# Thresholded attention and a feed-forward on one core: where q and k are loaded in SyncE's queue, and how the third pair's thresholds reach all partitions

## The chip, the core and the metric

The kernel runs on one core of a Trainium2 chip. Its engines work side by side, each through its own list of instructions in order: TensorE (PE; its weight loads are PEld), VectorE (DVE), ScalarE (ACT), GpSimd (POOL) and SyncE (SP), which here only issues DMAs. GpSimd issues DMAs too. An instruction waits for semaphores of others. The metric is the time of the whole program on the device in microseconds (us), the median of several runs.

## The reference

There are 8 batches of 8 heads, 576 rows of 64 each. For every head the scores are taken, all scores lower than the row's maximum minus tau are dropped, the rest go through a softmax, and the result is multiplied by v. The heads are put side by side (4608 rows of 512), and a feed-forward with a sigmoid gate follows.

```python
scores = scale * np.matmul(q, k.transpose(0, 1, 3, 2))
thresh = np.max(scores, axis=-1, keepdims=True) - tau
scores = np.where(scores >= thresh, scores, -1000000000.0)
attn = np.exp(scores - np.max(scores, axis=-1, keepdims=True))
attn = attn / (np.sum(attn, axis=-1, keepdims=True) + 1e-09)
attn_out = np.matmul(attn, v)            # then (B,H,S,D) -> (B*S, H*D) = x
h = x @ w_in                             # 512 -> 2048
g = h * (1.0 / (1.0 + np.exp(-1.702 * h)))
out = g @ w_out                          # 2048 -> 512
```

q, k, v are float32; the weights w_in and w_out come as 64-bit floats and are turned into float32 on the chip.

## The kernel before, in words

**Pairs.** Attention works on pairs of heads, 32 of them, 4 to a batch (`NPAIR` is 4, `n` the number of the pair). For pair `n`, `load_qk` brings q and k by four DMAs each into `raw0` and `raw1`, and `prep` transposes them on VectorE into `qkT` (L358). Each of these has one buffer for all pairs but 1 and 3, which have homes of their own in the arena, where the feed-forward will work later. So the load of a pair waits until the pair before it has been transposed. `scores` (L382 and, for the last 64 keys, L375) puts scores transposed into PSUM, keys on partitions, queries along the row, and `keep` (L405) copies them to SBUF on ScalarE, in four big tiles and one tail tile.

**Thresholds.** Queries lie along the row, so the maximum of a query goes over partitions. `in_groups` (L419) reduces within groups of 32 partitions, `over_tiles` and `over_groups` reduce the rest, and tau is taken off. The result must then stand on all 128 partitions, as `mb`, for the subtraction. There are two ways:

- For pairs below `BY_DMA` (8): `lower_rows` (L454, L459) forms a row in the small tile `flat`, `row_out` (L471) writes it to DRAM on SyncE's queue, and `row_in` (L480, L482) reads it back broadcast, once as `mb` and in two halves as `mbt` for the tail.
- For the others: `lower` (L443, L448) and `spread_max` (L463), a transpose of a broadcast operand on VectorE. There is no `mbt` then, and the subtraction of the tail is done in two halves (L494 instead of L491).

`sub` (L489) takes the thresholds off on VectorE, `mask` (L500) and `exps` (L504) follow on ScalarE. `values` multiplies by v (L518, tile `pv`). The sums are taken by TensorE too for the first five pairs (`sums_by_pe`, L518, tile `den`), else by VectorE. `spread_sums` and `place_x` (L585) scale and write the transposed result, `xT`.

**Weights.** w_in and w_out come in 16 pieces each, issued by GpSimd (L310, L311, 0.5 MB twice a piece) into staging places, w_in first. VectorE and ScalarE turn a piece into float32 (L321, L329, L335, L339, L347). The chain of loads goes on when a staging place is free.

**Feed-forward.** It takes blocks of 256 rows. The first two (L640, L622) can start when the four pairs of batch 0 are placed; all the others (L600, L690) use the seven products of Strassen's scheme, with sums made by GpSimd.

**Order.** The order of each engine's instructions is fixed while the program is built, by a planner. Every piece of work is a task with an engine, a planned cost, a rank, the tasks it comes `after` and the buffers it takes and gives. The planner plays time forward; a free engine takes the ready task with the lowest rank. The rank is the number of the pair plus a number of the function, `EARLY` for pairs 0 to 7 and `LATER` for the rest; the feed-forward's products have a rank behind all pairs. Planned costs have no effect but on this order. On the chip an instruction waits for what its data and buffers demand, not for the plan: an `after` without a transfer of data between the two tasks only sets their order where they lie on the same queue. Loads of q, k and v, both halves of the way through DRAM, and the stores of the output all lie on SyncE's one queue.

Of the kernel before, what the change touches and what calls it, by code (L numbers as in the profile page):

```python
# [30 lines left out]
def kernel(  # L31
# [37 lines left out]
    NPAIR = H // 2  # L69
# [59 lines left out]
    for x in ("raw0", "raw1", "qkT0", "qkT1", "mb"):  # L129
# [6 lines left out]
        "lower_rows": -1.89,  # L136
        "values": 1.63,
        "exps": 1.38,
        "load_qk": -1.15,
        "prep": -1.35,  # L140
        "load_v": 1.46,
        "mask": 0.88,
        "over_groups": -1.9,
        "sub": -0.29,
        "one_group": 0.95,
        "scores": -0.68,
        "spread_sums": 0.92,
        "sums_by_pe": 1.09,
        "in_groups": 0.61,
        "keep": -1.15,  # L150
    }
# [3 lines left out]
    }  # L155
    CV = {
        "cv_power": 0.15,
    }

    def task(engine, cost, rank, f, *a, after=(), take=(), give=(), lag=0.06):  # L160
        if 0 <= rank < LAST:
            rank += CV.get(f.__name__, 0.0) + (EARLY if a[0] < 2 * NPAIR else LATER).get(f.__name__, 0.0)
        tasks.append((engine, cost, rank, f, a, [x for x in after if x is not None],
                      take, give, lag))
        return len(tasks) - 1
# [67 lines left out]
    def own(n, *pools):  # L233
        return tuple(x + "_apart" for x in pools) if n in APART else pools
# [521 lines left out]


    BY_PE = 5
    BY_DMA = 8
    LEAD = 6  # L760
    WHOLE = 6

    FFU = 1.722

    W_IN, W_OUT = (3.21, 1.53), (3.16, 2.2)
    ready_w, w_loads = [], []
    for i in range(len(pieces)):
        if i < n_in:
# [11 lines left out]
        m = task("ACT", 0.79, rank, cv_power, i, after=[e])  # L780
# [6 lines left out]
    tau_done = task("DVE", 1.0, -2.0, tau_terms, after=[warm])  # L787


    placed, ffn = {}, []  # L790
    last_mm2, t_ready = {}, []

    def first_blocks():
# [88 lines left out]
    for n in range(NP):  # L882
        gate = per_pair * (n - LEAD)
        after = ffn[gate : gate + 1] if gate >= 0 else []
        r = float(n)

        slow = 1.2 if n < NPAIR else 1.0
        q0, q1 = (nc.sync, nc.scalar) if n == 0 else (nc.sync, nc.sync)
        lq = task("SP", 2.0, r - 2.0, load_qk, n, 0, q0, take=own(n, "raw0"), lag=2.0)
        lk = task("SP", 2.0 if n else 0.1, r - 2.0, load_qk, n, 1, q1, take=own(n, "raw1"), lag=2.0)  # L890
        v_tail = f"v_t{n % 2}"
        lv = task("SP", 2.1, r - 1.2, load_v, n, take=("v_m", v_tail), lag=2.0)
        pq = task("DVE", 0.77, r, prep, n, 0, after=[lq], take=own(n, "qkT0"), give=own(n, "raw0"))
# [8 lines left out]
        for t in range(NKT + 1):  # L902
            tail = t == NKT
            copies = []
            if tail or n >= WHOLE:
# [5 lines left out]
                    take=("psA", "s_t") if tail else ("psA", "psA") + own(n, "s_m"),  # L911
                    give=own(n, "qkT0", "qkT1") + ("kd",) if tail else (),
                )
                after = [a]
                copies = [task("ACT", 0.65, r, keep, n, t, c, after=[a], give=("psA",)) for c in cs]
            else:
                for c in range(2):
# [3 lines left out]
                        take=("psA",) + (own(n, "s_m") if c == 0 else ()),  # L921
                    )
                    after = [a]
# [1 line left out]
            mx.append(task("DVE", 0.76 if tail else 1.37, r, in_groups, n, t, ALU.max, after=copies))  # L925
        a = task("DVE", 0.78, r, over_tiles, n, ALU.max, after=mx)
        a = task("DVE", 0.78, r, over_groups, n, ALU.max, after=[a])
        if n < BY_DMA:
            a = task("DVE", 0.5, r, lower_rows, n, after=[a, tau_done], take=("row",))
            a = task("SP", 0.35, r, row_out, n, after=[a], lag=2.8)  # L930
            m = task(
                "SP", 1.5, r, row_in, n, after=[a], take=own(n, "mb") + ("mbt",), give=("row",),
                lag=5.0,
            )
        else:
            a = task("DVE", 0.7, r, lower, n, after=[a, tau_done])
            m = task("DVE", 1.38, r, spread_max, n, after=[a], take=own(n, "mb"))
        ws, subs = [], [m]
        for t in range(NKT + 1):
            tail = t == NKT  # L940
            a = task(
                "DVE", (0.76 if n < BY_DMA else 1.5) if tail else 1.36, r, sub, n, t, after=subs[-1:],
                give=own(n, "mb") + (("mbt",) if n < BY_DMA else ()) if tail else (),
            )
            subs.append(a)
            a = task("ACT", 0.68 if tail else 1.16, r, mask, n, t, after=[a])
            ws.append(task("ACT", 0.87 if tail else 1.34, r, exps, n, t, after=[a]))
        back = own(n, "s_m") * NKT + ("s_t",)
        every = range(NKT + 1)
        if n < NPAIR:  # L950

            pv = den = None
            for t in every:
# [3 lines left out]
                    take=("psM", "psM") if first else (),  # L957
# [3 lines left out]
                    take=("psA",) if first else (), give=(back[t],) if t < NKT else ("s_t", "v_m", v_tail),  # L961
# [60 lines left out]
```

## Time and profile before

| | before |
|---|---|
| time, median of 3 (lowest to highest) | 1401.76 us (1399.66 to 1402.35) |
| span of the profile | 1401.9 us |
| mean granted TensorE clock | 0.988 |
| PE busy before 140 us, and after | 89.4 us, 1251.8 us |
| VectorE busy over the span | 1037.4 us |
| ScalarE, GpSimd busy | 625.9 us, 281.7 us |
| first product of the feed-forward (L640) | 134.88 us |
| DMA over the span | 79.59 MB, 205728 packets |

In the profile "busy" is the time in which an engine has an instruction running. Lines of groups read: line of the code, engine, operation, output and input, shapes, number, then busy time and mean ns of one, then the idle time before them and what ended it. In a timeline a line is the start, the duration, the engine (SPq is SyncE's queue of DMA issues; the duration is that of the issuing, not of the transfer), and in brackets how long the engine had been idle and what it waited for. In the chain of waits a line is start, duration, and what held the end at that time.

### The profile page before, as it was taken

The numbers are of one execution on the slowest core, as the hardware profiler recorded it, in microseconds if no ns is written. First come the engines' busy times: TensorE is split into PE (matmuls) and PEld (weight loads), VectorE is DVE, ScalarE is ACT, GpSimd is POOL, SyncE is SP. The second block draws the span as 40 slices with busy tenths as digits, with TensorE's granted clock in tenths as the row PEclk, the third lists the DMA queues.
The fourth block names the chain that finished last, engine by engine and source line by source line (L and its number), as shares of the span: only waits on it lengthen the run. The fifth ranks groups of instructions, "written<-read, shape, count | busy, mean of one in ns | idle before, by whom it ended". The sixth has DMA issues, their size and how long they took to land.

```text
span 1401.9 us, 18089 instructions
## 1 busy us (share of the span) xinstructions
PE 1341.3 (96%) x6856; PEld 1012.6 (72%) x6856; DVE 1037.4 (74%) x1773; ACT 625.9 (45%) x806; POOL 281.7 (20%) x374
## 2 busy tenths in 40 slices
PE   5748999999999999999999999999999999999998
PEld 3325774467777777777777777777777778888887
DVE  7859899888888888878988888888888886111111
ACT  5647454654444545455454555543545453100100
POOL 1201223123021121212120303020212212211211
PEclk9869999999999999999999999999999999999999
DMA  8756873311111111111111111101111100000000
GB/s 181 202 176 193 248 250 92 92 25 27 41 27 41 26 34 33 26 33 26 41 26 41 24 35 26 41 17 41 26 42 26 25 9 8 8 16 15 1 15 15
DMA packets 205728, 79.59 MB, mean 57 GB/s; under 512 B 192841, under 2 KB 192841, under 8 KB 205641
## 3 DMA queue, kind: packets, MB, share of 16 engines
q1 hardware_dynamic: 196072, 44.60, 15.1%
q0 software_dynamic: 7200, 33.55, 7.1%
q8 instruction: 54, 0.88, 0.3%
q10 hardware_dynamic: 2368, 0.30, 0.2%
q14 instruction: 34, 0.27, 0.1%
HBM read 68.93 MB, written 9.47 MB: 56 GB/s over the span
## 4 chain that ended last, share of the span: by engine, by line
PE 86%; DVE 7%; DMA 4%; issue 2%; SPq 2%; ACT 0%; POOL 0%; DVEq 0%; POOLq 0%
PE hps L600 32%; PE ops L690 27%; PE pv L518 10%; PE ps L382 9%; PE ops L622 3%; PE ps L375 2%; SPq L246 2%; PE hps L640 1%; DVE s_m L489 1%; DVE part L419 1%; DMA w_out<-in_moe_w_in_dram 1%; DVE arena L489 1%; DMA arena<-row 1%; DMA arena<-in_moe_w_out_dram 1%; DMA w_out<-in_moe_w_out_dram 1%
## 5 line engine op out<-in xcount | busy, mean ns | idle before, releaser
L600 PE MATMUL hps<-xT,w_in 128*128 128x256 f32 x2048 | 457.3, 381 | 0.0
L600 PEld LDWEIGHTS hps<-xT,w_in 128*128 128x128 f32 x2048 | 385.8, 190 | 67.3 <-issue 11.3
L419 DVE TRANSPOSE_TENSOR_REDUCE part<-s_m 128x36 f32<-128x1152 f32 x228 | 304.8, 1355 | 61.6 <-ACT s_m L405 58.0
L405 ACT COPY s_m<-ps 128x576 f32<-128x576 f32 x240 | 141.1, 643 | 243.9 <-PE ps L382 240.6
L690 PE MATMUL ops<-w_out,arena 128*128 128x256 f32 x1024 | 232.8, 381 | 0.0
L690 PEld LDWEIGHTS ops<-w_out,arena 128*128 128x128 f32 x1024 | 192.8, 190 | 33.6 <-issue 6.2
L609 ACT ACTIVATE th<-hps 128x512 f32<-128x512 f32 x144 | 85.4, 593 | 294.2 <-PE hps L600 280.7
L500 ACT ACTIVATE s_m<-s_m 128x1152 f32<-128x1152 f32 x120 | 136.1, 1156 | 131.8 <-DVE s_m L489 131.0
L668 POOL TENSOR_TENSOR arena<-arena 128x256 f32<-128x256 f32 x64 | 58.5, 915 | 677.0 <-DVE arena L612 677.0
L690 PE MATMUL ops<-arena 128*128 128x256 f32 x768 | 174.3, 381 | 0.0
L489 DVE TENSOR_TENSOR s_m<-s_m,mb 128x1152 f32<-128x1152 f32 x120 | 160.9, 1374 | 16.5 <-DMA mb<-row 15.8
L612 DVE SCALAR_TENSOR_TENSOR arena<-th,hps 128x512 f32<-128x512 f32 x128 | 87.1, 680 | 111.3 <-ACT th L609 109.3
L690 PEld LDWEIGHTS ops<-arena 128*128 128x128 f32 x768 | 144.8, 190 | 24.7 <-issue 4.6
L382 PE MATMUL ps<-qkT 64*128 64x288 f32 x960 | 149.6, 435 | 10.9 <-DVE qkT L358 9.3
L504 ACT ACTIVATE s_m<-s_m,shift,scl 128x1152 f32<-128x1152 f32 x120 | 157.3, 1342 | 0.9
L382 PEld LDWEIGHTS ps<-qkT 64*128 64x128 f32 x960 | 84.2, 190 | 69.2 <-issue 32.2
L518 PE MATMUL pv<-s_m,v_m 128*64 128x288 f32 x960 | 123.1, 409 | 0.0
L712 DVE SCALAR_TENSOR_TENSOR osb<-ops,osb 128x256 f32<-128x256 f32 x112 | 44.5, 409 | 99.5 <-PE ops L690 98.5
L518 PEld LDWEIGHTS pv<-s_m,v_m 128*64 128x64 f32 x960 | 66.5, 137 | 53.0 <-issue 9.7
L622 PE MATMUL ops<-w_out,arena 128*128 128x512 f32 x128 | 59.4, 613 | 2.8 <-DVE w_out L347 2.8
L640 PE MATMUL hps<-xT,w_in 128*128 128x256 f32 x256 | 58.0, 383 | 3.5 <-DVE arena L646 2.5
L670 POOL TENSOR_TENSOR arena<-arena 128x256 f32<-128x256 f32 x64 | 60.3, 941 | 0.0
(97 smaller groups left out, 1050.3 us busy)
## 6 DMA issues: line engine op xcount, KB each, us to landing
out_dram<-osb SPq DMA_DIRECT2D x36, 256.0 KB, 2.0
q_raw<-in_q_dram SPq DMA_DIRECT2D x120, 72.0 KB, 2.2
k_raw<-in_k_dram SPq DMA_DIRECT2D x116, 72.0 KB, 2.2
v_m<-in_v_dram SPq DMA_DIRECT2D x64, 128.0 KB, 2.4
w_out<-in_moe_w_in_dram POOLq DMA_DIRECT2D x12, 512.0 KB, 9.6
arena<-in_moe_w_out_dram POOLq DMA_DIRECT2D x12, 512.0 KB, 6.0
w_out<-in_moe_w_in_dram POOLq DMA_DIRECT2D x12, 511.6 KB, 10.5
arena<-in_moe_w_out_dram POOLq DMA_DIRECT2D x12, 511.6 KB, 6.8
```

The source lines that it names most:

```text
L382: nc.tensor.matmul(ps[:, h, 0:SH], lhsT=kT[ts(h, D), ts(t, P)], rhs=qT[ts(h, D), ts(c, SH)], start=True, stop=True,)
L405: nc.scalar.copy(out=o, in_=pss.pop((n, t, c))[:, :, 0:SH])
L419: nc.vector.tensor_reduce(out=o, in_=i, axis=AXL.X, op=op, apply_transpose=True)
L489: nc.vector.tensor_tensor(out=s, in0=s, in1=mb, op=ALU.subtract)
L500: nc.scalar.activation(out=s, in_=s, func=AF.Prelu, alpha=STEEP)
L504: nc.scalar.activation(out=s, in_=s, func=AF.Exp, scale=scl, bias=shift)
L518: nc.tensor.matmul(o[c][ts(h, D), 0:SH], lhsT=lhsT, rhs=rhs, start=(t == 0), stop=(t == NKT),)
L600: nc.tensor.matmul(hidden[j][:, ts(f, BLK)], lhsT=w_in[:, c, ds((f * HF + j) * P, P)], rhs=xTs[blk][:, c, :], start=(c == 0), stop=(c == N ...
L609: nc.scalar.activation(out=ths[j], in_=hidden[j], func=AF.Tanh, scale=GELU_SCALE / 2)
L612: nc.vector.scalar_tensor_tensor(out=g[:, :, j, :], in0=two(ths.pop(j)), scalar=1.0, in1=two(hidden.pop(j)), op0=ALU.add, op1=ALU.mult,)
L622: nc.tensor.matmul(acc[i], lhsT=g0[:, j, ts(i, P)], rhs=w_out[:, j, :], start=(j == 0), stop=(j == NFC - 1),)
L690: nc.tensor.matmul(banks[k][:, ts(o, HM)], lhsT=left[:, j, :], rhs=right[:, j, :], start=(j == 0), stop=(j == HF - 1),)
```

## The change

Pair 2, the third, gets its thresholds by `spread_max` on VectorE instead of through DRAM. The loads of q and k of pair n, from pair 4 on, are planned after the thresholds of pair n-2, so that they lie behind these in SyncE's queue. It is meant to keep a long load from standing ahead of a small row that VectorE waits for. The planned cost of the loads of pairs 4 to 7 is raised, and the ranks are set anew for the first eight pairs and the weights.

```diff
     EARLY = {
         "lower_rows": -1.89,
         "values": 1.63,
         "exps": 1.38,
-        "load_qk": -1.15,
-        "prep": -1.35,
+        "load_qk": -1.72,
+        "prep": -1.69,
         "load_v": 1.46,
-        "mask": 0.88,
+        "mask": 1.64,
         "over_groups": -1.9,
-        "sub": -0.29,
+        "sub": -1.05,
         "one_group": 0.95,
-        "scores": -0.68,
-        "spread_sums": 0.92,
-        "sums_by_pe": 1.09,
+        "scores": 0.67,
+        "spread_sums": 1.4,
+        "sums_by_pe": 2.29,
         "in_groups": 0.61,
         "keep": -1.15,
     }
...
     CV = {
         "cv_power": 0.15,
+        "cv_frac": 0.13,
     }
...
-    BY_DMA = 8
+    BY_DMA = (0, 1, 3, 4, 5, 6, 7)
...
-    W_IN, W_OUT = (3.21, 1.53), (3.16, 2.2)
+    W_IN, W_OUT = (3.11, 1.53), (2.49, 2.62)
...
-    placed, ffn = {}, []
+    placed, spread, ffn = {}, {}, []
...
-        lq = task("SP", 2.0, r - 2.0, load_qk, n, 0, q0, take=own(n, "raw0"), lag=2.0)
-        lk = task("SP", 2.0 if n else 0.1, r - 2.0, load_qk, n, 1, q1, take=own(n, "raw1"), lag=2.0)
+
+        behind = [spread[n - 2]] if n >= NPAIR else []
+        cost = 3.5 if NPAIR <= n < 2 * NPAIR else 2.0
+        lq = task("SP", cost, r - 2.0, load_qk, n, 0, q0, after=behind, take=own(n, "raw0"), lag=2.0)
+        lk = task(
+            "SP", cost if n else 0.1, r - 2.0, load_qk, n, 1, q1, after=behind,
+            take=own(n, "raw1"), lag=2.0,
+        )
...
-        if n < BY_DMA:
+        if n in BY_DMA:
             a = task("DVE", 0.5, r, lower_rows, n, after=[a, tau_done], take=("row",))
             a = task("SP", 0.35, r, row_out, n, after=[a], lag=2.8)
...
             m = task("DVE", 1.38, r, spread_max, n, after=[a], take=own(n, "mb"))
+        spread[n] = m
```

The two other places that ask whether a pair's thresholds come by DMA, in the tail's `sub`, are changed likewise from `n < BY_DMA` to `n in BY_DMA`.

More of the change, by code (lines that the diff above doesn't have):

```diff
@@ L941 @@
             a = task(
-                "DVE", (0.76 if n < BY_DMA else 1.5) if tail else 1.36, r, sub, n, t, after=subs[-1:],
-                give=own(n, "mb") + (("mbt",) if n < BY_DMA else ()) if tail else (),
+                "DVE", (0.76 if n in BY_DMA else 1.5) if tail else 1.36, r, sub, n, t, after=subs[-1:],
+                give=own(n, "mb") + (("mbt",) if n in BY_DMA else ()) if tail else (),
             )
```

## The prediction

> **What bounds the kernel now.** I read the busy shares first, then the slices, then a table of stretches, then the chain of waits, then the two queues (VectorE and SyncE) around the one hole.
>
> ```profile
> span 1401.9 us, 18089 instructions
> PE 1341.3 (96%) x6856; PEld 1012.6 (72%) x6856; DVE 1037.4 (74%) x1773; ACT 625.9 (45%) x806; POOL 281.7 (20%) x374
> PE   5748999999999999999999999999999999999998
> DVE  7859899888888888878988888888888886111111
> ```
>
> The span is PE work plus PE idle: 1341.3 + 60.6. The digits put nearly all the idle into the first four slices, 140 us. The table of stretches says so in us (after the stretch: PE, PEld, DVE, ACT, POOL busy, granted clock, DMA share, GB/s):
>
> ```profile
> 0.00:60.00 60.00, 37.42 (x238) 21.68 (x240) 46.50 (x77) 40.17 (x52) 10.26 (x34) 0.94 0.75 175
> 60.00:70.00 10.00, 5.26 (x34) 2.69 (x30) 9.47 (x25) 3.04 (x6) 4.23 (x8) 0.91 1.10 286
> 70.00:80.00 10.00, 4.41 (x26) 1.94 (x24) 0.04 (x1) 0.95 (x2) 0.00 (x1) 0.84 1.04 334
> 80.00:90.00 10.00, 0.00 (x0) 0.00 (x0) 4.13 (x4) 2.64 (x3) 0.00 (x0) 0.50 0.53 123
> ...
> 140.00:230.00 90.00, 84.71 (x391) 60.39 (x390) 81.51 (x136) 48.75 (x63) 25.83 (x38) 0.99 0.73 220
> 230.00:300.00 70.00, 70.00 (x288) 32.58 (x288) 61.37 (x119) 33.24 (x41) 13.41 (x9) 0.99 0.24 63
> 300.00:1402.00 1102.00, 1097.13 (x5628) 869.00 (x5626) 786.32 (x1327) 458.24 (x592) 220.08 (x270) 1.00 0.12 26
> ```
>
> PE idles 50.6 us before 140, 5.3 from 140 to 230, nothing to 300 and 4.9 after. So the time is set by when the feed-forward starts (first L640 product at 134.88, a steady stream from 137.41, when pair 3's xT is written at 136.97), plus a nearly full PE. Before it, VectorE is the bound: up to 137.9 it is idle 31.7 us, of which 9.0 are the start (waits of 5.91 and 3.06), 3.43 one wait for pair 1's thresholds and 15.82 one for pair 2's. The chain of waits runs through that hole, SyncE's queue shows what fills it, and VectorE's row closes it:
>
> ```profile
> 70.90 7.29 SPq L246
> 78.30 3.77 DMA row<-flat
> 82.08 3.76 DMA mb<-row
> ```
> ```profile
> 59.22 4.04 SPq L246 DMA_DIRECT2D q_raw<-in_q_dram  x4
> 63.37 14.82 SPq L246 DMA_DIRECT2D k_raw<-in_k_dram  x4
> 78.30 0.53 SPq L471 DMA_DIRECT2D row<-flat  x1
> ```
> ```profile
> 62.35 0.23 DVE L459 STREAM_TRANSPOSE flat<-flat 32x64 f32<-32x64 f32 x1
> ...
> 85.87 5.16 DVE L489 TENSOR_TENSOR s_m<-s_m,mb 128x1152 f32<-128x1152 f32 x4 [15.82 <-DMA mb<-row]
> ```
>
> Pair 2's row is ready at 62.58 and goes out at 78.30: pair 5's q and k stand before it on SyncE, and their issues crawl (one takes 7.29 us; 490 ns is the usual) because the weights keep the DMA engines 104 to 110% busy there. Two trips through DRAM follow, 3.77 and 3.76. Pair 1 has the same on a small scale: its row is ready at 35.75 and leaves at 39.69, behind pair 4's k (12.95 us for four issues).
>
> **What the Trainium skill says.** "DMA: Bandwidth & Descriptors", section Anatomy of one DMA: a semaphore wait is done by the issuing sequencer ahead of the dispatch, and the engines just drain their queues. That fits: the small row DMA can't overtake the loads issued ahead of it, and two late DMAs cost their latencies one after the other. Same page, section Queues, rings and completion order: each engine goes round-robin between rows of work by packet; the trace agrees that rows share, as pair 5's k lands 12.5 us after issue in that stretch against 2.2 as the median. "VectorE: DVE Perf Modes", section The three transpose paths, has VectorE's transpose as 32x32 blocks; spread_max is one such instruction over 1152 columns, and the trace prices it: 1.37 us. "Perfetto Trace Analysis", section Optimization Strategy: in a kernel with several regimes the most-contended engine changes over time, and the gaps of the regime of interest are to be followed to the semaphore that ends them; here VectorE leads to 137 and PE after it, as the table shows.
>
> **The change part by part.**
>
> 1. Pair 2's thresholds by VectorE. Removed: the wait of 15.82, and 0.46 of lower_rows (0.231 + 0.232). Added on VectorE: lower 0.66 (0.229 + 0.252 + 0.176), spread_max 1.37, and a tail subtraction in two halves, 2 x 0.755 (median of L494) instead of 0.75. Together +0.20 + 1.37 + 0.76 = +2.33 us, all on the bound engine. It also takes pair 2's three broadcast reads off the DMA engines; I cost that at nothing, since nothing waits for it any more.
>
> 2. Loads of pair n >= 4 behind the thresholds of pair n-2. This is an order on the SyncE queue, not a new semaphore. Pair 4's loads go behind pair 1's row, so that row leaves at about 35.8 instead of 39.69, lands about 3.9 earlier, at 41.8, and VectorE comes for it at 42.1: the 3.43 wait goes. What is now queued behind a threshold is q and k of two pairs on, and behind these their transposes on VectorE (prep). Room for it in the trace: pair 4 is transposed at 58.42, its scores run only from 94.89; pair 5 at 119.96, 42 us after its last load was issued. In the later part SyncE waits 316 us in all for the raw buffers to come free anyway, and a pair takes about 36 us (one pv group to the next in the chain: 318.5, 354.1, 391.5), against some 5 to 10 for a load: nothing there.
>
> 3. Planned cost of the loads of pairs 4 to 7 3.5 instead of 2.0: only the plan, no instruction. Real times in the trace: 4.04 and 14.82, 9.75 and more under weight traffic, 2 without. The plan is nearer to the truth and still short of the bad ones.
>
> 4. New ranks (scores and sums later, subtractions, loads and transposes sooner, masks later; w_out pieces from 2.49 on instead of 3.16; cv_frac 0.13 later). No instruction is added, the order is shifted, for pairs 0 to 7 and the weights. Not seen in the trace, so from both sides. Best: 15 of 16 pieces of w_in are converted before 137 at 2.21 us each (0.42 + 0.43 + 0.69 + 0.67) and the first products need four; with all other eleven after the start it would come 24 earlier, of which perhaps half is usable, as the later products want them soon. But spread_sums of pair 3 moves behind more pieces (3.92 to 4.40), which speaks against it. Worst: scores of pairs 4 and 5, now done in PE's idle time, slide behind the start of the feed-forward: 2 x 5.66 (4.42 + 1.24 each) = 11.3. I take 0.
>
> 5. New small waits. With the hole closed, weights and thresholds are asked for sooner. DMA is 98.9 us busy before 137, so at a start near 120 it is 80% full: enough in sum, tight in places. The crowded stretch 150 to 170 shows what that looks like: five waits of VectorE on weights, 0.83 + 0.89 + 1.35 + 0.63 + 0.40 = 4.1. Bounds 0 to 8; I take 3.
>
> Sum: -15.82 - 3.43 + 2.33 + 3.0 = -13.9, on a VectorE path that sets the feed-forward's start. After the start PE is nearly full, so the earlier start passes to the end: 1401.8 - 13.9 = 1387.9, rounded **1388**. What could stop it from passing on is the last w_out piece: PE waits 2.81 for it at 227.4. The chain of weight loads stood still for 23.45 us in the hole (GpSimd waiting for a staging buffer), so it moves forward with the rest.
>
> **Rivals.**
>
> A. Half the gain is given back, by waits on q and k or on weights (5 to 8 more than I took), or by scores moved into PE's full stretch (5.7 to 11.3). For it: scores lose 1.35 in rank, and prep is planned 2 us after a load that can take 15. Against it: scores of pairs 4 and 5 are ready early in the trace, and any idle PE takes them. 1393 to 1399; middle **1396**. Chance 0.22.
>
> B. More than the sum, because the new order takes conversions off the road to the first product, 5 to 12 more. For it: eleven pieces aren't needed yet. Against: rank of spread_sums. **1379**. Chance 0.14.
>
> C. A new hole of the size of the old. The most likely place is VectorE waiting in order at prep of pair 4 or 5 for a load that crawls; all behind it, subtractions and weights, waits too. For it: the loads are started later than before and their issue took 19 us (4.04 + 14.82, pair 5) and 21 (9.75 + 6.38 + 5.22, pair 6) in full traffic. 17 + one wait of 18 to 20: 1402 to 1408, **1405**, slower. Against: loads leave the fullest stretch, 60 to 80, for 85 to 105, where DMA is at 0.32 to 0.5. Chance 0.10.
>
> D. The hole is hidden: something else sets the start, such as weights. Then within 0.2%, **1401**. Against: 15 pieces are there by 137 and four are needed, and PE and VectorE both stand in the hole. Chance 0.04.
>
> **How the numbers follow.** The forecast has 0.50, spread over 1383 to 1392. Faster takes forecast, A and B and nearly all their edges: 0.86; same 0.04; slower 0.10. The range holds the forecast (0.50), A to its far end (0.22) and the nearer half of B (0.07), 0.79 together: 1376 to 1399.
>
> **What would show it.** Right: the wait of VectorE for mb from row, 15.8, is gone, and there are 25 spread_max instead of 24; pair 1's row leaves within 1 us after its transpose; first L640 near 120; PE idle before it down to about 35; the stretch after the start as full as now. Wrong: a wait of VectorE for q_raw or k_raw over 5 us; L382 products of pairs 4 and 5 behind the first L640; a longer wait of L622 for w_out.

## The result, and the profile after

The changed kernel takes 1392.73 us (median of 4 runs, 1391.75 to 1397.4) beside 1401.63 for the kernel before: the ratio, that of the mean times as in all that follows, is 0.9945, 95% interval 0.9921 to 0.997. It is faster by 8.9 us by the medians, where 13.9 was forecast. The profiled execution spans 1391.0 us; that of the kernel before was longer than its median (1403.66 us, a span of 1401.9), so the two profiles lie 10.9 us apart.

From the page of the changed kernel, the span, the busy shares and two rows of slices:

```profile
span 1391.0 us, 18051 instructions
PE 1341.9 (96%) x6856; PEld 1015.6 (73%) x6856; DVE 1053.8 (76%) x1776; ACT 634.4 (46%) x806; POOL 295.7 (21%) x374
PE   5778999999999999999999999999999999999999
DVE  7989999978888888889888888888888887111111
```

VectorE's row has no dip in its third slice any more, and PE's third slice went from 4 to 7. The table of stretches, in the same columns as before:

```profile
0.00:60.00 60.00, 40.88 (x254) 25.20 (x256) 49.26 (x84) 42.00 (x53) 11.12 (x34) 0.91 0.78 193
60.00:70.00 10.00, 5.06 (x38) 2.73 (x35) 9.75 (x20) 9.90 (x10) 1.06 (x2) 0.87 0.69 146
70.00:80.00 10.00, 10.00 (x61) 5.09 (x60) 9.61 (x15) 6.32 (x10) 3.19 (x6) 0.79 0.73 238
80.00:90.00 10.00, 9.55 (x65) 4.72 (x62) 9.50 (x24) 5.29 (x9) 3.19 (x6) 1.00 0.86 294
...
140.00:230.00 90.00, 87.15 (x413) 56.71 (x411) 83.92 (x141) 49.68 (x64) 25.45 (x35) 1.00 0.69 219
230.00:300.00 70.00, 63.55 (x251) 34.38 (x251) 60.84 (x97) 32.57 (x37) 10.99 (x8) 0.95 0.30 67
300.00:1402.00 1102.00, 1087.57 (x5584) 860.68 (x5582) 786.80 (x1323) 461.11 (x589) 232.93 (x269) 1.00 0.12 26
```

VectorE is busy 9.61 and 9.50 us from 70 to 90, where it had 0.04 and 4.13. But 230 to 300, which was full for PE, now lacks 6.45. (The span ends at 1391.0, so the last stretch has 1091 us, not 1102.) PE's idle time, from these tables and the whole stretch to 140 (103.60 busy):

| us | before | after | difference |
|---|---|---|---|
| PE idle to 140 | 50.6 | 36.4 | -14.2 |
| 140 to 230 | 5.3 | 2.9 | -2.4 |
| 230 to 300 | 0 | 6.45 | +6.45 |
| 300 to the end | 4.8 | 3.4 | -1.4 |
| PE busy, whole span | 1341.3 | 1341.9 | +0.6 |

The sum is -10.9, the difference of the two spans. So before 140 us PE gained what was forecast, and after 230 us a new wait took nearly half of it back. In SyncE's queue (start, duration of the issues) the rows leave at once, and the loads come behind them (line numbers shift by up to six from run to run, as the edits add lines):

```profile
37.36 0.28 SPq L472 DMA_DIRECT2D row<-flat  x1
...
46.85 2.22 SPq L247 DMA_DIRECT2D q_raw<-in_q_dram  x4
49.11 11.52 SPq L247 DMA_DIRECT2D k_raw<-in_k_dram  x4
...
88.02 0.30 SPq L472 DMA_DIRECT2D row<-flat  x1
92.42 0.35 SPq L481 DMA_DIRECT2D arena<-row  x1
```

Pair 1's row goes 0.3 us after its transpose starts (37.10, 0.23 long). Pair 4's k is still slow, 11.52 for its four issues, but nothing that VectorE needs soon stands behind it. What VectorE waits for in its place, by its own timeline, is small:

```profile
96.03 5.16 DVE L490 TENSOR_TENSOR arena<-arena 128x1152 f32<-128x1152 f32 x4 [1.40 <-DMA arena<-row]
...
103.57 0.78 DVE L359 STREAM_TRANSPOSE qkT<-q_raw 128x576 f32<-128x576 f32 x1 [1.72 <-DMA q_raw<-in_q_dram]
105.59 0.78 DVE L359 STREAM_TRANSPOSE qkT<-k_raw 128x576 f32<-128x576 f32 x1 [1.24 <-DMA k_raw<-in_k_dram]
```

The new wait of PE is this, first in VectorE's timeline, then in GpSimd's, then in PE's:

```profile
269.11 0.18 DVE L438 COPY fold<-red 64x36 f32<-64x36 f32 x1
269.33 2.24 DVE L439 TENSOR_TENSOR red<-red,fold 64x36 f32<-64x36 f32 x1
271.60 2.27 DVE L438 COPY fold<-red 32x36 f32<-32x36 f32 x1
273.90 2.27 DVE L439 TENSOR_TENSOR red<-red,fold 32x36 f32<-32x36 f32 x1
276.21 2.79 DVE L558 TENSOR_SCALAR r<-red 32x18 f32<-32x18 f32 x4
...
280.21 0.95 DVE L586 TENSOR_TENSOR xT<-pv,rc 128x192 f32<-128x192 f32 x4
```
```profile
269.12 4.71 POOL L664 TENSOR_TENSOR arena<-w_out,arena 128x1024 f32<-128x1024 f32 x2
273.78 4.64 POOL L664 TENSOR_TENSOR w_out<-w_out 128x1024 f32<-128x1024 f32 x2
```
```profile
281.31 2.29 PE L383 MATMUL ps<-qkT 64*128 64x288 f32 x8 [6.45 <-DVE xT L586]
283.53 3.11 PE L623 MATMUL ops<-w_out,arena 128*128 128x512 f32 x4
```

Tiny operations of VectorE, which take 0.17 to 0.19 elsewhere (four of L558 together 0.71), last as long as one of GpSimd's sums of w_out, 2.3 us, each; of the four of L558, by their total of 2.79, only one can. They belong to pair 7's sums; pair 7 is placed some 8 us late (2.24 + 2.27 + 2.27 + 2.79, less the 1.25 they take alone), and PE stands for 6.45: the next scores wait for a PSUM place that pair 7's `place_x` (L586) gives back. The granted clock is 1.00 from 269 to 275, 0.83 from 275 to 281 and 0.60 from 281 to 287, and the next twelve products take 2.29 + 3.11 where the same ones take 1.24 + 1.98 before the wait: 2.2 more. The Trainium skill has it in "SBUF — State Buffer", section SBUF: two separate sides: VectorE and GpSimd share a pair of ports under an exclusive lock, held for a whole instruction; the forms of VectorE that need the pair are those with two inputs in SBUF (against a GpSimd instruction that reads SBUF) and those in a mode that uses two ports. These rows agree in length, 2.24 to 2.27 beside sums of 2.3, and L439, with its two inputs, is of the first form; in which mode the copies and scalar operations ran, the trace doesn't say.

### The profile page after: what moved, and what is told of

It is laid out like the page before. It is cut to its first block, busy times and chain, and to the rows that moved or that the text cites. A ratio compares the mean times of both kernels' runs of the same rounds, so it can differ in the third digit from the quotient of the medians.

```text
span 1391.0 us, 18051 instructions
## 1 busy us (share of the span) xinstructions
PE 1341.9 (96%) x6856; PEld 1015.6 (73%) x6856; DVE 1053.8 (76%) x1776; ACT 634.4 (46%) x806; POOL 295.7 (21%) x374
## 4 chain that ended last, share of the span: by engine, by line
PE 85%; DVE 9%; DMA 2%; SPq 1%; issue 1%; ACT 0%; POOL 0%; DVEq 0%; ACTq 0%; POOLq 0%
PE hps L601 32%; PE ops L691 28%; PE pv L519 9%; PE ps L383 8%; PE hps L641 4%; DVE part L420 2%; PE ps L376 2%; DVE s_m L490 1%; SPq L247 1%; PE den L519 1%; DMA arena<-in_moe_w_out_dram 1%; DVE arena L340 1%; DVE red L439 1%; DMA v_m<-in_v_dram 1%; DVE w_in L348 0%
## 5 line engine op out<-in xcount | busy, mean ns | idle before, releaser
L601 PE MATMUL hps<-xT,w_in 128*128 128x256 f32 x2048 | 457.5, 381 | 0.0
L691 PEld LDWEIGHTS ops<-w_out,arena 128*128 128x128 f32 x1024 | 192.3, 190 | 36.1 <-issue 10.4
L669 POOL TENSOR_TENSOR arena<-arena 128x256 f32<-128x256 f32 x64 | 52.0, 812 | 610.8 <-DVE arena L613 610.8
L490 DVE TENSOR_TENSOR s_m<-s_m,mb 128x1152 f32<-128x1152 f32 x120 | 180.3, 1540 | 0.8
L691 PE MATMUL ops<-arena 128*128 128x256 f32 x768 | 171.0, 379 | 0.0
L613 DVE SCALAR_TENSOR_TENSOR arena<-th,hps 128x512 f32<-128x512 f32 x128 | 85.8, 671 | 100.9 <-ACT th L610 100.9
L676 POOL TENSOR_TENSOR arena<-arena 128x512 f32<-128x512 f32 x32 | 62.6, 1963 | 111.2 <-PE ops L691 111.2
L671 POOL TENSOR_TENSOR arena<-arena 128x256 f32<-128x256 f32 x64 | 60.1, 938 | 0.0
```

The costliest lines, as they stand in the source:

```text
L490: nc.vector.tensor_tensor(out=s, in0=s, in1=mb, op=ALU.subtract)
L601: nc.tensor.matmul(hidden[j][:, ts(f, BLK)], lhsT=w_in[:, c, ds((f * HF + j) * P, P)], rhs=xTs[blk][:, c, :], start=(c == 0), stop=(c == N ...
L613: nc.vector.scalar_tensor_tensor(out=g[:, :, j, :], in0=two(ths.pop(j)), scalar=1.0, in1=two(hidden.pop(j)), op0=ALU.add, op1=ALU.mult,)
L676: nc.gpsimd.tensor_tensor(out=u, in0=a12, in1=u, op=ALU.subtract)
L691: nc.tensor.matmul(banks[k][:, ts(o, HM)], lhsT=left[:, j, :], rhs=right[:, j, :], start=(j == 0), stop=(j == HF - 1),)
```

## The experiments

The loads and ranks are named as in the change. The ratio is to the kernel before, run beside each, with its 95% interval; start is that of the first feed-forward product on PE (L640 in the kernel before), in the one profiled execution of each run. The planner makes the order anew for every run: e1 to e4 differ from the kernel before, e7 and e8 from the changed kernel and e12 from e9 in the places of many other tasks too, on TensorE as well. Only e5 and e6 keep the order of the changed kernel on every engine, and e9, e10 and e11 those of e2, e1 and e4, but for the added copies. With the same order the start still differs by 0.5 to 3.4 us (123.14, 125.67 and 122.24; 121.45 and 124.73; 128.87 and 128.35; 136.26 and 137.47), so smaller differences of the start say nothing.

| run | what | us | ratio | interval | start |
|---|---|---|---|---|---|
| after | the change | 1392.73 | 0.9945 | 0.9921 to 0.997 | 123.14 |
| e1 | both parts, old ranks | 1388.5 | 0.9902 | 0.9887 to 0.9917 | 128.87 |
| e2 | VectorE alone, old ranks | 1387.0 | 0.99 | 0.988 to 0.992 | 121.45 |
| e3 | order of loads alone, old ranks | 1390.58 | 0.9916 | 0.9901 to 0.9931 | 124.78 |
| e4 | new ranks alone | 1416.68 | 1.0104 | 1.0086 to 1.0123 | 136.26 |
| e5 | the change, later sums | 1384.37 | 0.9874 | 0.9858 to 0.9891 | 125.67 |
| e6 | e5, first sums later too | 1385.11 | 0.9879 | 0.9864 to 0.9895 | 122.24 |
| e7 | the change without VectorE's part | 1403.7 | 1.0011 | 1.0003 to 1.0019 | 129.88 |
| e8 | the change without the order of loads | 1396.21 | 0.9954 | 0.994 to 0.9969 | 121.89 |
| e9 | e2, later sums | 1390.8 | 0.9924 | 0.9911 to 0.9937 | 124.73 |
| e10 | e1, later sums | 1397.88 | 0.9974 | 0.9966 to 0.9983 | 128.35 |
| e11 | e4, later sums | 1405.8 | 1.0035 | 1.0022 to 1.0049 | 137.47 |
| e12 | e9, pair 1 by VectorE too | 1399.65 | 0.9988 | 0.998 to 0.9997 | 128.51 |

### Which part makes the gain: e1 to e4

e1 is the kernel before with everything of the change but the ranks:

```diff
-    BY_DMA = 8
+    BY_DMA = (0, 1, 3, 4, 5, 6, 7)
...
+        behind = [spread[n - 2]] if n >= NPAIR else []
+        cost = 3.5 if NPAIR <= n < 2 * NPAIR else 2.0
```

> The kernel before with pair 2 spread by VectorE and the loads behind the thresholds, ranks as before. Theory Q (the queue makes the gain: the row no longer stands behind a load): both waits of VectorE on rows (15.8 and 3.4) are gone, the first L640 product comes at 120 to 125 instead of 134.9, the time is 1385 to 1393. Theory R (the new ranks make it): the start stays at 133 or later, 1397 or more.

The two waits on rows are gone and the time is as expected, but the start is not: 128.87. VectorE waits for loads instead, as its timeline shows for pair 5 (and 3.40 more for pair 4's k):

```profile
109.18 0.78 DVE L358 STREAM_TRANSPOSE qkT<-q_raw 128x576 f32<-128x576 f32 x1 [6.30 <-DMA q_raw<-in_q_dram]
111.19 0.78 DVE L358 STREAM_TRANSPOSE qkT<-k_raw 128x576 f32<-128x576 f32 x1 [1.23 <-DMA k_raw<-in_k_dram]
```

10.9 us together: the wait that the prediction's rival C had, at half its size. e1 is faster than the whole change all the same: PE idles 41.5 us before 140 (36.4 in the changed kernel), but nothing is lost from 230 to 300, where PE is full.

e2 has the first part of that diff alone:

```diff
-    BY_DMA = 8
+    BY_DMA = (0, 1, 3, 4, 5, 6, 7)
```

> The kernel before with pair 2 spread by VectorE alone; loads and ranks as before. Theory Q: the wait of 15.8 is gone, that of pair 1 (3.4) stays, 2.3 us of VectorE work are added: start at 124 to 128, time 1388 to 1395. Theory R: start at 133 or later, 1397 or more.

0.99, a little better than expected; start 121.45. Pair 1's wait is there as expected, 3.64. So this one part makes as much as both.

e3 has the other part alone:

```diff
+        behind = [spread[n - 2]] if n >= NPAIR else []
+        cost = 3.5 if NPAIR <= n < 2 * NPAIR else 2.0
```

> The kernel before with the loads behind the thresholds alone; pair 2 goes through DRAM still, ranks as before. Theory Q: pair 2's row leaves within 2 us of its transpose, and what VectorE waits for it falls from 15.8 to 0 to 5, pair 1's 3.4 goes: start at 119 to 127, time 1384 to 1394, so that the spreading by VectorE isn't needed for most of the gain. Rival: pair 4's load, now late, stops VectorE at its transpose in turn, for 5 or more: 1394 to 1402. Theory R: 1397 or more.

0.9916, start 124.78. Pair 2's row leaves at 59.44, yet VectorE waits 8.00 for it, more than expected: the trip through DRAM itself takes long in the weights' traffic (59.44 to 73.65; the DMA share is 1.01 from 59 to 74). SyncE's queue, and VectorE's row:

```profile
59.44 0.30 SPq L471 DMA_DIRECT2D row<-flat  x1
65.78 0.36 SPq L480 DMA_DIRECT2D mb<-row  x1
```
```profile
73.65 5.17 DVE L489 TENSOR_TENSOR s_m<-s_m,mb 128x1152 f32<-128x1152 f32 x4 [8.00 <-DMA mb<-row]
```

e1, e2 and e3 overlap in their intervals: the two parts are two cures of one hole, and their gains don't add.

e4 has the ranks alone (`EARLY`, `CV`, `W_IN`, `W_OUT` as in the change):

```diff
-        "scores": -0.68,
+        "scores": 0.67,
...
-    W_IN, W_OUT = (3.21, 1.53), (3.16, 2.2)
+    W_IN, W_OUT = (3.11, 1.53), (2.49, 2.62)
```

> The kernel before with the new ranks alone. Theory Q: loads of pair 4 or 5 still lie ahead of rows of pairs 1 and 2, a wait of VectorE on a row of 8 or more remains; 1396 to 1406. Theory R: the waits are filled with other work, start at 128 or earlier, 1385 to 1393.

Slower by 1.04%, worse than either theory had. The hole is where it was, in VectorE's timeline of this run:

```profile
82.32 5.17 DVE L490 TENSOR_TENSOR s_m<-s_m,mb 128x1152 f32<-128x1152 f32 x4 [15.62 <-DMA mb<-row]
```

and the same four small operations take 2.24, 2.26, 2.28 and 2.79 beside GpSimd's sums; PE waits 6.35, and the granted clock is 0.91 from 230 to 300.

### The collision: e5 and e6

e5 makes the third and fourth sum wait for pair 7:

```diff
     def t_sum(x, k):
         o, a, b = (y[:, ts(k, 4), :] for y in T_SUMS[x])
+        if (x, k) == (2, 0):
+            nc.gpsimd.tensor_copy(out=late, in_=xTs[2][:, NPAIR - 1, 128:129])
...
+        if n == 2 * NPAIR - 1:
+            tasks[t_ready[4]][5].append(placed[n])
```

> The changed kernel with one GpSimd instruction more: ahead of the third and fourth of the sums of w_out (L664) it copies one column of xT that pair 7's place_x writes, so these sums can't run before pair 7 is placed; every other instruction and its order as in the changed kernel. Theory C (GpSimd's sums at 269 to 278 hold up VectorE's small operations of pair 7, four of them at 2.2 to 2.8 us instead of 0.2 to 0.7, and so PE for 6.45): these operations take 0.2 again, pair 7 is placed 8 to 9 earlier, the PE wait of 6.45 and the slow clock behind it go: 6 to 9 less than the changed kernel, 1382 to 1387. Rival S (PE would wait there anyway, for scores moved behind the start, or VectorE is late by itself): 0 to 2 less.

1384.37: 8.4 less than the changed kernel, and the intervals are apart (0.9858 to 0.9891, and 0.9921 to 0.997). VectorE's timeline, and GpSimd's under it:

```profile
271.50 0.19 DVE L440 TENSOR_TENSOR red<-red,fold 64x36 f32<-64x36 f32 x1
...
272.14 0.71 DVE L559 TENSOR_SCALAR r<-red 32x18 f32<-32x18 f32 x4
...
275.88 1.38 DVE L421 TRANSPOSE_TENSOR_REDUCE part<-s_m 128x36 f32<-128x1152 f32 x1 [0.86 <-ACT s_m L407]
278.96 1.38 DVE L421 TRANSPOSE_TENSOR_REDUCE part<-s_m 128x36 f32<-128x1152 f32 x1 [1.71 <-ACT s_m L407]
```
```profile
274.79 4.67 POOL L667 TENSOR_TENSOR arena<-w_out,arena 128x1024 f32<-128x1024 f32 x2
```

The small operations are back at 0.19 and 0.71. The sums now lie beside transposing reductions, which take 1.38 as they do alone: this kind isn't held up. PE is full from 230 to 300, as the stretch says:

```profile
230.00:300.00 70.00, 70.00 (x288) 39.76 (x285) 61.29 (x107) 39.16 (x46) 13.21 (x10) 1.00 0.29 67
```

The start was 2.5 later in this execution than in that of the changed kernel, at the same order, and the median is still the shortest of all runs (that of e6 beside it within the noise). The two profiled executions are 6.6 us apart, of which the wait is 6.45; the 8.4 of the medians also takes in what these two don't show.

e6 does the same with the first two sums:

```diff
+        if (x, k) == (0, 0):
+            nc.gpsimd.tensor_copy(out=late, in_=w_out[:, NFC - 1, 0:1])
```

> As the run before, and the first two sums also wait, by a copy of one column of the last piece of w_out, until that is converted. Theory C: L336 and L340 of the last piece take 0.4 and 0.7 instead of 2.60 and 2.73 and the wait of L623 for it (1.61) goes: 1 to 3 less than the run before. Rival: the sums then hold up other VectorE work right behind it, and nothing is won: within 1 of it.

The wait for the last piece of w_out is gone, but two of L432 and one of L439 of a pair take 3.83 and 2.28 in turn (0.36 and 0.18 alone), and PE waits 3.20 there. 0.9879 and 0.9874: nothing won.

### The change less one part: e7 and e8

e7 is the change with `BY_DMA` over all eight pairs again (the comparisons read `n < BY_DMA` as before):

```diff
-    BY_DMA = (0, 1, 3, 4, 5, 6, 7)
+    BY_DMA = 8
```

> The changed kernel with pair 2 through DRAM again; loads behind the thresholds and new ranks stay. If spreading by VectorE does a needed part: the row's two trips in the weights' traffic (up to 3.8 each) stop VectorE for 3 to 8 and pair 4's load comes that much later, 1394 to 1401. If the order in the queue is enough: VectorE saves 2.3, 1386 to 1393.

1.0011, slower than expected, and by about 0.1% slower than the kernel before. The waits are of the kinds named, in VectorE's timeline:

```profile
68.36 5.17 DVE L490 TENSOR_TENSOR s_m<-s_m,mb 128x1152 f32<-128x1152 f32 x4 [5.88 <-DMA mb<-row]
...
104.32 5.17 DVE L490 TENSOR_TENSOR arena<-arena 128x1152 f32<-128x1152 f32 x4 [3.03 <-DMA arena<-row]
```

with 1.99 + 1.71 for pair 4's q and k between; start 129.88, and the collision is there too (PE waits 5.06). With the new ranks the change wins nothing without VectorE's part.

e8 takes the order of the loads out of the change:

```diff
-        lq = task("SP", cost, r - 2.0, load_qk, n, 0, q0, after=behind, take=own(n, "raw0"), lag=2.0)
+        lq = task("SP", 2.0, r - 2.0, load_qk, n, 0, q0, take=own(n, "raw0"), lag=2.0)
```

(and `lk` likewise).

> The changed kernel with the loads free to go ahead of the thresholds again (and at the old planned cost); pair 2 by VectorE and new ranks stay. Theory Q: a wait on a row behind a load comes back, for pair 1 (k of pair 4 lies right behind row 0, ahead of row 1) at 3 to 8 us: 1393 to 1402. If the order in the queue does nothing beside the spreading: within 3 of the changed kernel.

Pair 1's wait comes back, 3.18, but the waits for q and k go, and the start is the same, 121.89. 0.9954 and 0.9945 overlap: no worth of this part is to be seen beside the other.

### Can the sums be put later anywhere: e9 to e12

The same copy (the diff of e5) on e2, e1 and e4. These runs were on another chip than e1 to e8; the kernel before took 1401.51 there and 1402.04 beside e1 to e4, so differences of times between the two carry about 0.5 us of that.

> The run with pair 2 spread by VectorE alone and the ranks as before, with the one GpSimd copy ahead of the third sum that makes these sums wait for pair 7. There four operations of L557 took 9.34 us beside the sums at 255 to 265, and PE waited 3.49. Theory C: these take 0.7 and PE's 3.49 goes: 1382 to 1385, the best so far. If the collision only moves: 1386 to 1389.

Not faster than e2: 0.9924 to 0.99, and the intervals overlap a little, so a loss isn't shown either. In e2, VectorE's timeline had

```profile
255.44 9.34 DVE L557 TENSOR_SCALAR r<-red 32x18 f32<-32x18 f32 x4
```

and in e9 that is 0.71, but right behind pair 7 this order has subtractions, with two operands in SBUF; VectorE's row, and PE's:

```profile
284.99 9.03 DVE L490 TENSOR_TENSOR s_m<-s_m,mb 128x1152 f32<-128x1152 f32 x3
```
```profile
294.67 9.01 PE L601 MATMUL hps<-xT,w_in 128*128 128x256 f32 x32 [5.62 <-DVE arena L613]
```

Three take 9.03 where they take 3.9 alone, the gate behind them (L613) is late, and PE waits 5.62 where it waited 3.49. The collision has moved.

> The run with both parts and the ranks as before, with the same copy. There the sums stood beside reductions, and PE had no idle time from 230 to 300. Theory C: nothing to win, 1387 to 1390 (this shows that the copy has no worth of its own). Otherwise 1385 or less.

Missed: 1397.88, 9.4 more than e1. Here the copy turned sums that stood beside reductions into sums beside subtractions: PE waits 5.87 for L613 at 301, its clock is 0.83 from 300 to 320, and from 140 to 230 it idles 3.5 instead of 1.4. VectorE's row, and PE's:

```profile
286.71 12.49 DVE L490 TENSOR_TENSOR s_m<-s_m,mb 128x1152 f32<-128x1152 f32 x4
```
```profile
301.41 6.48 PE L601 MATMUL hps<-xT,w_in 128*128 128x256 f32 x16 [5.87 <-DVE arena L613]
```

The two profiled executions differ by 11.5 us in their spans: PE idles 8.1 longer, 5.9 of it this wait, and is busy 3.4 longer at the same number of products. The four subtractions take 12.49 where four take 5.2 alone. The 2.1 from 140 to 230 lie ahead of the copy, at the same order, so they aren't its doing. The copy isn't neutral; where the sums fall decides.

> The run with the new ranks alone, with the same copy. There small operations took 2.24, 2.26, 2.28 and 2.79 beside the sums, PE waited 6.35, and its clock was 0.91 from 230 to 300 and 0.90 to 320. Theory C (the collision makes the new ranks slower): 6 to 14 less, 1403 to 1411. If the new ranks lose by something else: 1414 or more.

10.9 less, as expected, and still 0.35% slower than before: the collision is the larger part of what the new ranks cost alone. Of the 10.4 between the two profiled spans 4.7 are PE's idle time and 5.7 its busy time, at a clock of 0.98 from 230 to 300 where it had 0.91. VectorE's wait for pair 2's row is still there, 17.0 in this run. What makes up the 0.35% beside the kernel before, which has that wait too, wasn't settled.

e12 is e9 with pair 1 by VectorE too:

```diff
-    BY_DMA = (0, 1, 3, 4, 5, 6, 7)
+    BY_DMA = (0, 3, 4, 5, 6, 7)
```

> As the first run of this call, with the thresholds of pair 1 by VectorE too. This takes away VectorE's wait of 3.6 for pair 1's row and adds 2.33 us of work: by these numbers 1 less, 1381 to 1384. If the added work isn't the whole price, or the wait only moves: 1385 to 1390.

Missed by 15: 1399.65. Start 128.51 instead of 124.73, and the wait moved to pair 3's row, as the list of VectorE's waits says (total, times, longest):

```profile
DVE arena L490 <- DMA arena<-row: 8.0, 1, 8.0
```

The collision of e9 is there as well (PE waits 5.64 for L613). The order of many tasks differs here from e9's; which of them costs the rest wasn't tried.

## Why the prediction was right, and where its size was off

**The bound and the hole: right.** PE idle at the start, VectorE as what leads there, and pair 2's row behind pair 5's loads. Either way of keeping VectorE from that wait (e2, e3) gives 0.8 to 1.0% alone, and the ranks without them lose 1.0% (e4).

**Parts 1 and 2: right, but they don't add as two gains.** The wait of 15.82 and that of 3.43 are gone in the changed kernel. What the prediction didn't say is that either part alone closes most of the hole, and that the 3.43 needn't be a net gain: without the order of loads (e8) pair 1's wait is back at 3.18, the waits for q and k are gone, and the start is no later. The VectorE work added is as priced where it can be seen (pair 2's L495 1.51 for both halves, L464 1.38).

**Part 5, new small waits:** 3.0 were taken; 1.40 + 1.72 + 1.24 = 4.4 were measured on VectorE. Rival C's wait is real: 10.9 in e1, 7.5 of it for pair 5's loads, whose issues take 9.75 and 4.71.

**The start:** near 120 was named, 123.14 came. PE idle before 140 fell by 14.2, where the sum had 13.9. That these agree is in part luck. In e1, which has both parts and not the ranks, it fell by only 9.1 (50.6 to 41.5), so in the changed kernel the ranks, taken at 0, won some 5 us before the start, more than runs of one order differ by. e2, with VectorE's part alone and the old ranks, came as far (an idle time of 35.3).

**The step that failed is the one behind the start:** "After the start PE is nearly full, so the earlier start passes to the end", together with part 4, the ranks, "I take 0". The term mis-sized is part 4: 0 was taken, and behind the start it cost +6.45 of PE waiting. By the profiles the sum then reads -14.2 before 140, +6.45, -2.4 and -1.4 in the other stretches and +0.6 of busy time in all, in which the 2.2 of slow clock are contained. e5 takes the collision away and gains 8.4. It came with the new ranks: the same four slow operations stand in all of the changed kernel, e4, e7 and e8, though the old ranks have one of their own in e2 (9.34, PE waiting 3.49). By e1 beside the change, 0.9902 to 0.9945, the new ranks cost 0.4% (the intervals are just apart). With the sums where they do no harm on either side, e1 and e5, it is 0.9902 to 0.9874, and the intervals overlap a little: apart from the collision the ranks aren't shown to lose.

The 1392.73 measured lies between the forecast's stretch (1383 to 1392) and rival A's (1393 to 1399, chance 0.22). A had half of the gain given back, which is near to what came, but by other causes. Scores of pairs 4 and 5 would move behind the start; they still begin ahead of it (85.77 to 92.33 and 115.48 to 122.06). Or the small waits would be 5 to 8 longer than taken; they were 1.4 longer.

The trace of before held a hint, in its VectorE timeline:

```profile
220.11 2.60 DVE L335 TENSOR_SCALAR arena<-arena 128x512 int32<-128x512 int32 x1
222.75 2.73 DVE L339 SCALAR_TENSOR_TENSOR arena<-arena 128x512 int32<-128x512 int32 x1
```

In the piece just ahead the same two take 0.42 and 0.69; these two lie beside the first of the same sums (GpSimd, 220.00 to 224.93). The prediction saw only the wait for the last piece of w_out there, not that an order that puts small operations beside these sums can pay the same.

## What to carry to other kernels

When a small transfer that an engine waits for shares a queue with bulk loads, look at what is issued ahead of it; here freeing it by order and by another way around the queue was one gain, not two. An earlier start passes to the end only if the order behind it meets no new collision: here two engines that were both off the bound held each other up, and then the bound. Moving one of them helped where its new neighbours were of a kind that isn't held up (8.4 us in e5), and cost about as much where they were of one that is (9.4 in e10; in e9 nothing clear of the noise). So what a new order is worth shows only with its collisions away: the new ranks lost 0.4% with theirs, and aren't shown to lose without it.

## What the runs showed that was not expected

- A reordering by ranks alone moved the time by +1.04% and, with one GpSimd copy more, by +0.35%: one instruction was worth 10.9 us.
- Beside GpSimd's sums (2.3 us each) VectorE's operations on 32 or 64 partitions by 18 or 36 took 2.24 to 2.29 each instead of 0.17 to 0.19, four scalar ones up to 9.34 instead of 0.71, and subtractions 9.03 for three instead of 3.9; transposing reductions kept their 1.38.
- The row's trip through DRAM, out of SBUF and a broadcast back, takes about 5 us at its shortest: 1.2 from the row's issue to that of the read behind it (37.36 to 38.59 in the changed kernel, with a DMA share of 0.52 from 37 to 43), and 3.5 to 4.0 until the read has landed. Under the weights' loads in e3 (1.01) the row was issued at 59.44, the read at 65.78, and VectorE went on at 73.65: 14.2, though the last issue ahead of the row in its queue had ended at 51.3.
